# Small products of the late runs of tokens placed further behind their DVE steps in a fused gated scan and top-1 expert layer

## The chip, the cores and the metric

One core of a Trainium2 chip runs the whole kernel. The metric is the device time of one execution in microseconds (us). Engines: PE is TensorE (PEld are its weight loads), DVE is VectorE, ACT is ScalarE, POOL is GpSimd, SP is SyncE, which here only issues DMAs (SPq in the rows).

## What is computed

Inputs are x, r_gate and i_gate of 4 x 5056 x 256 floats, a modality per token, and 8 experts with w1 (256 x 1024) and w2 (1024 x 256).

```python
# gated scan over time, for each of 4 batches and 256 channels
a_t = exp(8 * sigmoid(r_gate) * log(a_base))
x_gated = sqrt(max(1 - a_t * a_t, 1e-6)) * sigmoid(i_gate) * x
h = a_t[:, t] * h + x_gated[:, t];  y[:, t] = h          # t = 0..5055
# top-1 experts on the 20224 rows of y
logits = y @ w_gate + modality_bias[modality_id]
e = argmax(logits);  gate = softmax(logits)[e]
out = gate * (relu(y @ w1[e]) @ w2[e])
```

## The kernel before

**Two stages that overlap.** The first stage goes over 23 runs of time steps (`CHUNKS`, numbered 0 to 22; runs 4 to 20 have 256 steps, that is 1024 tokens over the four batches). For each run it loads the three inputs, does the scan, finds a power of two that scales the run's rows into f16 (`size_chunk`, "scale"), splits the scaled rows into a high and a low f16 half (`split_chunk` on ACT, `low_parts` on DVE), multiplies by the gate weights ("logits", at the end of `low_parts`), finds each token's expert and its rank among that expert's tokens (`route_chunk`, "ranks"), transposes the rows by DMA (`rows_part`, line 858) and scatters them by POOL into the experts' lists in HBM (line 1043). The second stage takes pages of 256 rows of the two likeliest experts, and a few pages of 128, back from there (tile X, line 1280), multiplies them by w1 (L1371, into ph), makes relu halves H on ACT (L1302) and on DVE (L1304), multiplies by w2 (L1411, into po), scales on ACT (L1323) and scatters the output by POOL (L1327). The main products stand on PE in groups of twelve of 128 x 256; a page of 256 rows has four groups into ph and four into po, so one H step of DVE goes with two groups. There are 654 such groups in all.

**The small products.** Each run has few of them on PE, and each one sits between DVE steps. Scale: DVE makes `mxy` (L774); PE turns it into psz (L633); DVE reduces psz (`m1y`, L636) and makes `dmy` (L640); PE spreads that (L644, L646); DVE makes the scales `scy` (L653) from `miy` (L649), and ACT's and DVE's split wait for these. Logits: the last DVE low step (L817), then sixteen products (L830), then DVE `lt` (L889) and the steps of routing. Ranks: DVE `cu` (L922), then three products (L927 to L930), then DVE `dt` (L934). psz and psl, the PSUM tiles of scale and of logits with ranks, share two buffers (tag `lg`).

**What sets the order.** Every engine works through its own queue in program order. The order is written while the kernel is built, by a planner (`run`) that has a cost for every step. A piece of work is a generator; it asks for an engine, a duration, a condition and a lag, and the step that it asked for is put in the queue of the engine when the planner's clock of that engine reaches it. The lag of a request is the least time in the plan between the end of this step and the start of the *next* step of the same generator; without one it is 0.1 (same engine) or 0.2 (another engine):

```python
lag = th.req[3] if len(th.req) > 3 else None
th.req = next(th.gen, None)          # puts the step into its queue
th.t += (0.1 if th.req[0] == eng else 0.2) if lag is None else lag
```

So the lag on a request for PE holds back the DVE step that reads the product, and the lag on a DVE request holds back the product that follows it. Runs 7 and 8 and later ones have 3.0 for the lag between L633 and `m1y` and between L644 and `miy` (`SIZE_LAG`), and 3.0 between the last low step and the logits, between `cu` and the ranks and between the ranks and `dt` (`LAG`). Between `mxy` and L633 and between `dmy` and L644 there is no lag but the 0.2.

Of the kernel before, what the change touches and what calls it, by code (L numbers as in the profile page):

```python
# [49 lines left out]
C_STEP = 2.89  # L50
GROW = 1.01
SIZE_LAG = 3.0
EARLY = 7
URGENT = 0.03
ROW_STEP = 2.4
LAG = 3.0
# [21 lines left out]
def place(kind, c):  # L78

    return BASE[kind] + C_STEP * c + (RANK[kind][c] if c < len(RANK[kind]) else 0.0)  # L80
# [7 lines left out]
def columns(c):  # L88

    return B * CHUNKS[c][1] // P  # L90
# [16 lines left out]
def kernel(  # L107
# [161 lines left out]
    def seen(*names):  # L269
        return allof(*[lambda n=n: mark.get(n, FAR) for n in names])  # L270

    def room(tag, k=1):

        def at():
            d = slots[tag]
            old = [n - d.bufs for n in range(d.n, d.n + k) if n >= d.bufs]
            return max((d.back.get(n, FAR) for n in old), default=0.0)
        return at

    def take(tag):  # L280
        slots[tag].n += 1
        return slots[tag].n - 1

    def give(tag, n):
        slots[tag].back[n] = plan["end"]

    def allof(*fs):
        def at():
            t = 0.0
            for f in fs:  # L290
                t = max(t, f())
                if t >= FAR:
                    break
            return t
        return at
# [6 lines left out]
    def add(gen, prio, t=0.0, urgent=False):  # L302

        th = Thread(gen, prio, t, urgent)
        if th.req is not None:
            threads.append(th)
# [258 lines left out]
    def done(c, name):  # L565

        give(*tickets[c, name])
# [62 lines left out]
    def power_of_two(name, mx, ng, ps, sc, iv, lag=None):  # L630

        yield "PE", 0.1, None, lag
        nc.tensor.matmul(ps[0:ng, 0:P], mx, identb, start=True, stop=True)  # L633
        yield "DVE", 0.2, None
        m1 = sm.tile([4, 1], F32, name=f"m1{name}", tag="m1")
        nc.vector.tensor_reduce(out=m1[0:ng], in_=ps[0:ng, 0:P], axis=AX.X, op=ALU.max)  # L636
        yield "DVE", 0.14, None
        dm = sm.tile([4, 5], BF16, name=f"dm{name}", tag="dm")
        nd = ng if ng == 1 else ng + 1
        nc.vector.tensor_scalar(  # L640
            out=dm[0:ng, 0:nd], in0=identx[0:ng, 0:nd], scalar1=m1[0:ng], scalar2=None, op0=ALU.mult
        )
        yield "PE", 0.1, None, lag
        nc.tensor.matmul(ps[:, P : P + ng], onesb[0:ng, :], dm[0:ng, 0:ng], start=True, stop=True)  # L644
        if nd > ng:
            nc.tensor.matmul(ps[:, P + ng : P + nd], quad, dm[:, ng:nd], start=True, stop=True)  # L646
        yield "DVE", 0.1, None
        mi = sm.tile([P, 5], I32, name=f"mi{name}", tag="mi")
        nc.vector.tensor_scalar(  # L649
            out=mi[:, 0:nd], in0=ps[:, P : P + nd].bitcast(I32), scalar1=EBITS, scalar2=None, op0=ALU.bitwise_and  # L650
        )
        yield "DVE", 0.1, None, 0.0
        nc.vector.scalar_tensor_tensor(  # L653
            out=sc.bitcast(I32), in0=mi[:, 0:ng], scalar=6.0 * TWO23, in1=s256[:, 0:ng], op0=ALU.max, op1=ALU.subtract,
            reverse1=True,
        )
        yield "DVE", 0.1, None, 0.0
        nc.vector.tensor_scalar(
            out=iv.bitcast(I32), in0=mi[:, nd - 1 : nd], scalar1=6.0 * TWO23, scalar2=-4.0 * TWO23, op0=ALU.max, op1=ALU.add,
        )  # L660
# [75 lines left out]
    def modality_bias(c):  # L736

        C = columns(c)
        yield "POOL", 0.3 + 0.03 * C, seen(("modality", c))
        shc = [P, C, E]  # L740
        mc = slice(COL[c], COL[c + 1])
        bm = sm.tile([P, C, E], F32, name=f"bm{c}", tag="bm", bufs=3)
        bn = sm.tile([P, C, E], F32, name=f"bn{c}", tag="bn")
        mul = lambda o, a, m: nc.gpsimd.tensor_tensor(
            out=o, in0=a[:, mc].broadcast_to(shc), in1=mb[:, m : m + 1, :].broadcast_to(shc), op=ALU.mult
        )
        mul(bm, mf, 1)
        mul(bn, mg, 0)
        nc.gpsimd.tensor_tensor(out=bm, in0=bm, in1=bn, op=ALU.add)
        tiles["bm", c] = bm  # L750
        mark["bias", c] = plan["end"] + 0.2

    def size_chunk(c):

        t0, T = CHUNKS[c]
        z = T / 256
        yield "DVE", 0.07 + 2.13 * z, seen(("load", c, "x"))
        xg = tiles[c][2].rearrange("p (h g t) -> p h g t", h=2, g=B)
        top = sm.tile([P, B], F32, name=f"top{c}", tag="top", bufs=4)
        nc.vector.tensor_reduce(  # L760
            out=top, in_=xg.rearrange("p h g t -> p g h t"), axis=AX.XY, op=ALU.max, apply_absolute_value=True
        )
        mark["peak", c] = plan["end"] + 0.2
        mx = sm.tile([P, 4], BF16, name=f"mxy{c}", tag="mxy", bufs=4)
        grow = GROW * T ** 0.5
        if c:
            yield "DVE", 0.12, seen(("scan", c - 1))
            lm = sm.tile([P, B], F32, name=f"lm{c}", tag="lm")
            nc.vector.tensor_reduce(
                out=lm, in_=tiles["last", c - 1].rearrange("p h g o -> p g (h o)"), axis=AX.X, op=ALU.max,  # L770
                apply_absolute_value=True,
            )
            yield "DVE", 0.1, None
            nc.vector.scalar_tensor_tensor(out=mx, in0=top, scalar=grow, in1=lm, op0=ALU.mult, op1=ALU.add)  # L774
        else:
            yield "DVE", 0.1, None
            nc.vector.tensor_scalar(out=mx, in0=top, scalar1=grow, scalar2=None, op0=ALU.mult)
        yield "SP", 0.0, allof(room("lg"), seen("gate")), 0.0
        lag = SIZE_LAG if c > 6 else SIZE_LAG / 3 if c > 1 else None
        tl = take("lg")  # L780
        ps = psl.tile([P, 512], F32, name=f"psz{c}", tag="lg")
        sc = sm.tile([P, 4], F32, name=f"scy{c}", tag="scy", bufs=4)
        iv = sm.tile([P, 1], F32, name=f"ivy{c}", tag="ivy", bufs=4)
        yield from power_of_two(f"y{c}", mx, B, ps, sc, iv, lag)
        give("lg", tl)
        yield "DVE", 0.1, None, 0.0
        ivl = sm.tile([P, 1], F32, name=f"ivl{c}", tag="ivl", bufs=4)
        nc.vector.tensor_tensor(out=ivl, in0=iv, in1=ivg, op=ALU.mult)
        tiles["iv", c] = iv, ivl
        tiles["sc", c] = sc  # L790
        mark["sized", c] = plan["end"] + 0.2

    def split_chunk(c):
# [6 lines left out]
        ys = a.rearrange("p (s h k g b) -> p s h g k b", s=2, h=2, g=B, b=Q)  # L800
        add(low_parts(c, yg, ys, sc), (0, place("low", c)), plan["end"], urgent=c < EARLY)
        add(modality_bias(c), (0, place("low", c)), plan["end"])
# [7 lines left out]
    def low_parts(c, yg, ys, sc):  # L810

        t0, T = CHUNKS[c]
        z = T / 256
        lag = LAG if c > 6 else None
        for g in range(B):
            yield "DVE", 0.14 + 0.52 * z, seen(("high", c, g)), 0.0 if g < B - 1 else lag
            nc.vector.scalar_tensor_tensor(  # L817
                out=ys[:, 1, :, g], in0=yg[:, :, g, :].rearrange("p h (k b) -> p h k b", b=Q), scalar=sc[:, g : g + 1],
                in1=ys[:, 0, :, g], op0=ALU.mult, op1=ALU.subtract,
            )  # L820
        mark["split", c] = plan["end"] + 0.2
        done(c, "g")
        yield "PE", 0.35 + 0.35 * z, room("lg"), 1.25 if c > 6 else 0.0
        tl = take("lg")
        ps = psl.tile([P, 512], F32, name=f"psl{c}", tag="lg")
        tiles["ps", c] = tl, ps
        mm = [(s, h) for s in range(2) for h in range(2)]
        for m, (s, h) in enumerate(mm):
            for g in range(B):
                nc.tensor.matmul(  # L830
                    ps[Q * g : Q * g + Q, 0:T], wg16[:, h, :], ys[:, s, h, g], start=(m == 0), stop=(m == len(mm) - 1),
                )
        mark["lg", c] = plan["end"]
        y_free(c)
# [46 lines left out]

    def route_chunk(c):
        C = columns(c)
        lag = LAG if c > 6 else None
        small = 0.1 + 0.014 * C
        yield "DVE", 0.07 + 0.27 * C / 8, seen(("lg", c), *([("oh", c - 1)] if c else []))
        ticket, ps = tiles["ps", c]
# [19 lines left out]
        nc.vector.tensor_tensor(out=l, in0=l, in1=mx.broadcast_to(sh), op=ALU.subtract)  # L907
        add(gates(c, l), (0, place("gates", c)), plan["end"] + 0.2, urgent=c < EARLY)
        yield "DVE", small, None
# [513 lines left out]
    def start_chunk(c):  # L1423
        early = c < EARLY
        add(load_chunk(c), (0, place("load", c)))
# [91 lines left out]
```

## Time and profile before

| what | value |
|---|---|
| median of three runs | 968.93 us (964.12 to 969.37) |
| the profiled execution, its own time | 970.96 us |
| its span, first to last instruction | 969.2 us |
| mean granted TensorE clock | 0.988 |
| busy: PE, PEld, DVE, ACT, POOL | 909.6, 787.4, 650.7, 578.6, 427.8 us |

Busy times are of the span; what lies around it is 1.8 us. Matmuls are pipelined, so a PE that is shown busy all the time can still do less than its peak; a wait of PE shows as idle time in front of an instruction, with the instruction that ended it. "PEclk" in tables by stretch is the granted clock, 1.00 for 2.4 GHz.

### The profile page before, as it was taken

How to read it: one execution, taken by the hardware profiler on the slowest of the kernel's cores; microseconds unless marked ns; L12 is line 12 of the kernel's file. 1: busy time of each engine (PE TensorE's matmuls, PEld its weight loads, DVE VectorE, ACT ScalarE, POOL GpSimd, SP SyncE). 2: the span in 40 equal slices, each digit the busy share in tenths (PEclk: the TensorE clock that was granted, in tenths of full speed). 3: DMA queues.
4: the chain of work that ended last, by engine and by line, in shares of the span. 5: the costliest groups of instructions: out<-in, count | busy, mean ns of one | idle time of the engine just before them, and what ended most of it. 6: DMA issues, size and time to landing. Idle time of an engine off the chain costs nothing. (4 is left out here: it accounts for less than half of the span.)

```text
span 969.2 us, 22535 instructions
## 1 busy us (share of the span) xinstructions
PE 909.6 (94%) x8518; PEld 787.4 (81%) x8518; DVE 650.7 (67%) x1665; ACT 578.6 (60%) x819; POOL 427.8 (44%) x550
## 2 busy tenths in 40 slices
PE   3968998998999999998999999999999999999996
PEld 2556787787888888887888888888998988888886
DVE  7978988688898788798979876973352332233321
ACT  8978667696768766866787676843233333333332
POOL 6434356345456555544555555444443212112112
PEclk9998999899999999999999999999999999999999
DMA  9587798889779888998988887643732222122110
GB/s 317 155 221 207 178 215 263 184 211 246 226 164 218 183 230 210 230 204 179 232 228 221 209 196 202 138 94 93 175 106 72 53 51 60 45 51 60 45 40 19
DMA packets 227992, 155.85 MB, mean 161 GB/s; under 512 B 197857, under 2 KB 201058, under 8 KB 227874
## 3 DMA queue, kind: packets, MB, share of 16 engines
q1 hardware_dynamic: 211554, 110.35, 51.0%
q0 software_dynamic: 16176, 43.98, 13.5%
q8 instruction: 68, 1.11, 0.5%
q14 instruction: 50, 0.41, 0.2%
q10 hardware_dynamic: 144, 0.00, 0.0%
HBM read 68.76 MB, written 44.35 MB: 117 GB/s over the span
## 5 line engine op out<-in xcount | busy, mean ns | idle before, releaser
L1371 PE MATMUL ph<-X,hw 128*128 128x256 f16 (+1 forms) x3840 | 469.3, 273 | 14.8 <-DMA X<-rows 14.1
L1411 PE MATMUL po<-hw,H 128*128 128x256 f16 x3840 | 473.9, 274 | 6.0 <-ACT H L1302 4.8
L1371 PEld LDWEIGHTS <-hw 128*128 128x128 f16 x3936 | 377.3, 98 | 64.4 <-DMA X<-rows 11.3
L1411 PEld LDWEIGHTS <-H 128*128 128x128 f16 x3864 | 374.5, 98 | 54.4 <-ACT H L1302 5.5
L1304 DVE SCALAR_TENSOR_TENSOR H<-ph,H 128x512 f16<-128x512 f32 (+1 forms) x332 | 219.9, 668 | 246.1 <-ACT H L1302 244.8
L1302 ACT ACTIVATE H<-ph 128x512 f16<-128x512 f32 (+1 forms) x332 | 190.8, 581 | 255.1 <-PE ph L1371 253.1
L1327 POOL DMA_INDIRECT out_dram<-ot,mt x161 | 178.3, 1107 | 276.7 <-ACT ot L1323 238.2
L1043 POOL DMA_INDIRECT rows<-rt,di x158 | 178.2, 1128 | 225.5 <-PE ph L1371 86.8
L1323 ACT ACTIVATE ot<-po,gt 128x256 f32<-128x256 f32 x161 | 76.1, 473 | 74.3 <-PE po L1411 72.1
L622 DVE TENSOR_TENSOR_SCAN g<-a,g 128x512 f32<-128x512 f32 (+1 forms) x78 | 94.8, 1227 | 0.5
L605 DVE SCALAR_TENSOR_TENSOR g<-x,g 128x1024 f32<-128x1024 f32 (+1 forms) x40 | 48.4, 1209 | 24.2 <-ACT x L600 24.2
L817 DVE SCALAR_TENSOR_TENSOR a<-g,scy,a 128x512 f16<-128x512 f32 (+2 forms) x92 | 60.0, 676 | 4.7 <-ACT a L805 4.7
L805 ACT ACTIVATE a<-g,scy 128x512 f16<-128x512 f32 (+2 forms) x92 | 56.3, 656 | 4.4 <-DVE scy L653 4.4
L594 ACT ACTIVATE a<-a,ch 128x1024 f32<-128x1024 f32 (+2 forms) x46 | 50.9, 1118 | 0.1
L588 ACT ACTIVATE a<-a 128x2048 f32<-128x2048 f32 (+2 forms) x23 | 38.4, 1671 | 20.2 <-DMA a<-in_r_gate_dram 20.1
L579 DVE SCALAR_TENSOR_TENSOR g<-g,x 128x1024 f32<-128x1024 f32 (+1 forms) x40 | 48.0, 1200 | 0.1
L760 DVE TENSOR_REDUCE top<-x 128x4 f32<-128x2048 f32 (+2 forms) x23 | 45.3, 1971 | 3.7 <-DMA x<-in_x_dram 3.7
L573 ACT ACTIVATE g<-g 128x2048 f32<-128x2048 f32 (+2 forms) x23 | 38.4, 1668 | 13.1 <-DMA g<-in_i_gate_dram 13.0
L598 ACT ACTIVATE x<-a 128x2048 f32<-128x2048 f32 (+2 forms) x23 | 38.4, 1669 | 11.2 <-DVE g L579 7.1
L600 ACT ACTIVATE x<-x,quarter 128x2048 f32<-128x2048 f32 (+2 forms) x23 | 40.6, 1763 | 0.3
L600 ACT ACT_TABLE_LOAD x22 | 28.2, 1283 | 0.4
L1043 POOL DMA_INDIRECT rows<-nt,ni x16 | 15.8, 990 | 20.8 <-PE ph L1371 9.2
(210 smaller groups left out, 463.5 us busy)
## 6 DMA issues: line engine op xcount, KB each, us to landing
a<-in_r_gate_dram SPq DMA_DIRECT2D x38, 512.0 KB
g<-in_i_gate_dram SPq DMA_DIRECT2D x38, 512.0 KB
x<-in_x_dram SPq DMA_DIRECT2D x38, 512.0 KB
wr<-in_moe_w_dram SPq DMA_DIRECT2D x4, 1024.0 KB
out_dram<-ot,mt POOLq DMA_INDIRECT x161
rows<-rt,di POOLq DMA_INDIRECT x158
cr<-in_moe_w_dram SPq DMA_DIRECT2D x2, 1024.0 KB
rt<-a SPq DMA_TRANSPOSE x92
```

The costliest lines, as they stand in the source:

```text
L594: nc.scalar.activation(sl, sl, AF.Exp, scale=ch[:, h : h + 1], bias=ch[:, h : h + 1])
L600: nc.scalar.activation(s, s, AF.Sqrt, scale=-0.25, bias=quarter)
L622: nc.vector.tensor_tensor_scan(out=gi, data0=ai, data1=gi, initial=0.0, op0=ALU.mult, op1=ALU.add)
L805: nc.scalar.activation(ys[:, 0, :, g], yg[:, :, g, :].rearrange("p h (k b) -> p h k b", b=Q), AF.Copy, scale=sc[:, g : g + 1])
L817: nc.vector.scalar_tensor_tensor(out=ys[:, 1, :, g], in0=yg[:, :, g, :].rearrange("p h (k b) -> p h k b", b=Q), scalar=sc[:, g : g + 1], i ...
L1043: ins = nc.gpsimd.indirect_dma_start(out=rows[:, :], out_offset=bass.IndirectOffsetOnAxis(ap=idx, axis=0), in_=src, in_offset=None, bounds ...
L1302: nc.scalar.activation(t.H[:, 0, hs, :], ph[:, :, 0:st], AF.Relu)
L1304: nc.vector.scalar_tensor_tensor(out=t.H[:, 1, hs, :], in0=ph[:, :, 0:st], scalar=0.0, in1=t.H[:, 0, hs, :], op0=ALU.max, op1=ALU.subtract,)
L1323: nc.scalar.activation(t.ot[:, a, :], po, AF.Copy, scale=t.gt[:, a : a + 1])
L1327: ins = nc.gpsimd.indirect_dma_start(out=out[:, :], out_offset=bass.IndirectOffsetOnAxis(ap=t.mt[:, a, 0:1], axis=0), in_=t.ot[:, a, :], i ...
L1371: ins = nc.tensor.matmul(ph[:, v, 0:st], lhsT, rhs, start=(m == 0), stop=(m == len(mm) - 1))
L1411: ins = nc.tensor.matmul(po, lhsT, rhs, start=(f == 0 and m == 0), stop=(f == NF - 1 and m == len(mm) - 1))
```

## The change

From run 9 on, the lag behind each scale product becomes 12.0 in place of 3.0, and the lag on the last low step, on `cu` and on the rank products becomes 6.0 in place of 3.0. No instruction of PE, DVE, POOL or SP is added or taken away; ACT has 43 table loads in place of 47 in its queue, by the order in which its functions follow each other.

```diff
 SIZE_LAG = 3.0
+SIZE_LATE = 12.0
+LATE = 9
+LAG_LATE = 6.0
...
-        lag = SIZE_LAG if c > 6 else SIZE_LAG / 3 if c > 1 else None
+        lag = SIZE_LATE if c >= LATE else SIZE_LAG if c > 6 else SIZE_LAG / 3 if c > 1 else None
...
-        lag = LAG if c > 6 else None
+        lag = LAG_LATE if c >= LATE else LAG if c > 6 else None
...
-        lag = LAG if c > 6 else None
+        lag = LAG_LATE if c >= LATE else LAG if c > 6 else None
```

Lines of the changed kernel are 3 higher than those of the kernel before (L1304 is L1307). Up to run 9's `m1y` on DVE all queues are the same. Counted in PE's queue, this many groups of main products stand ahead of the products of a run, before and after:

| run | L633 | L644 | logits | ranks |
|---|---|---|---|---|
| 9 | 121, 121 | 128, 136 | 144, 156 | 153, 167 |
| 10 | 137, 137 | 144, 155 | 162, 188 | 170, 197 |
| 13 | 203, 211 | 206, 225 | 223, 245 | 236, 256 |
| 16 | 267, 295 | 270, 305 | 288, 326 | 301, 337 |
| 17 | 289, 322 | 292, 339 | 311, 372 | 318, 383 |
| 18 | 313, 349 | 317, 362 | 333, 380 | 340, 388 |
| 19 | 335, 350 | 338, 362 | 356, 389 | 361, 401 |
| 22 | 401, 436 | 405, 446 | 414, 462 | 419, 469 |

Page 26 starts behind group 200 and page 30 behind group 232 in both. Between `mxy` of run 9 and `mxy` of run 16 DVE's queue holds 73 H steps before and 87 after; from run 16 to run 19 it holds 34 and 27, from run 19 to run 22 32 and 43.

DVE's queue at run 9's `m1y` (the reduction of the first scale product; g9 is run 9's scan tile, H16 and H17 are pages 16 and 17, cu8 and b8 belong to run 8), before:

```order
L922 SCALAR_TENSOR_TENSOR cu8_3934<-rmask8_189,oh8_3917 128x64
L636 TENSOR_REDUCE m1y9_3952<-psz9_3885 4x1
L605 SCALAR_TENSOR_TENSOR g9_3161<-x9_3225,g9_3161 128x1024
L1304 SCALAR_TENSOR_TENSOR H16_3865<-ph16_0_3866,H16_3865 128x512
L1304 SCALAR_TENSOR_TENSOR H16_3865<-ph16_1_3921,H16_3865 128x512
L1032 TENSOR_REDUCE sg8_3994<-ex8_3957 128x8
```

and after:

```order
L967 TENSOR_REDUCE b8_4156<-bh8_4151 1x2
L1307 SCALAR_TENSOR_TENSOR H17_4041<-ph17_1_4088,H17_4041 128x512
L639 TENSOR_REDUCE m1y9_4160<-psz9_3885 4x1
L763 TENSOR_REDUCE top10_4175<-x10_3738 128x4
L1307 SCALAR_TENSOR_TENSOR H17_4041<-ph17_2_4135,H17_4041 128x512
L643 TENSOR_SCALAR dmy9_4228<-identx_171,m1y9_4160 4x5
```

`m1y` of run 9 moved back by 31 rows, behind the rest of run 9's scan, and `dmy` went with it.

DVE's queue ahead of run 16's `mxy` (a15 and g15 are run 15's tiles; L817 and L820 are the low steps, L760 and L763 the peak of x), before:

```order
L817 SCALAR_TENSOR_TENSOR a15_6269<-g15_6545,scy15_6900,a15_6269 128x16x32
L1304 SCALAR_TENSOR_TENSOR H33_7151<-ph33_2_7238,H33_7151 128x512
L817 SCALAR_TENSOR_TENSOR a15_6269<-g15_6545,scy15_6900,a15_6269 128x16x32 x3
L1304 SCALAR_TENSOR_TENSOR H33_7151<-ph33_3_7280,H33_7151 128x512
L760 TENSOR_REDUCE top16_7338<-x16_7190 128x4
L1304 SCALAR_TENSOR_TENSOR H34_7317<-ph34_0_7318,H34_7317 128x512
L1315 TENSOR_SCALAR gt33_7377<-mt33_6743,hiv1_230 128x2
L1142 TENSOR_TENSOR d36_7380<-b13_6751,u_136 1x2
L769 TENSOR_REDUCE lm16_7382<-last15_7233 128x4
```

and after:

```order
L1307 SCALAR_TENSOR_TENSOR H36_7547<-ph36_1_7585,H36_7547 128x512
L1307 SCALAR_TENSOR_TENSOR H36_7547<-ph36_2_7646,H36_7547 128x512
L1307 SCALAR_TENSOR_TENSOR H36_7547<-ph36_3_7681,H36_7547 128x512
L1318 TENSOR_SCALAR gt36_7761<-mt36_7304,hiv0_229 128x2
L1307 SCALAR_TENSOR_TENSOR H37_7732<-ph37_0_7733,H37_7732 128x512
L1307 SCALAR_TENSOR_TENSOR H37_7732<-ph37_1_7769,H37_7732 128x512
L763 TENSOR_REDUCE top16_7814<-x16_7694 128x4
L1307 SCALAR_TENSOR_TENSOR H37_7732<-ph37_2_7801,H37_7732 128x512
L652 TENSOR_SCALAR miy15_7850<-psz15_7290 128x5
L772 TENSOR_REDUCE lm16_7855<-last15_7607 128x4
```

The low steps of run 15 moved from ahead of run 16's peak to behind run 16's `mxy`, and H steps of the pages stand alone there.

SP's queue at the load of page 26 (X26; rt11 and rt10 are transposes of runs 11 and 10, a13, g13 and x13 the loads of run 13), before:

```order
L1281 DMA mt25_5241<-rows_78 128x2x2
L858 DMA_TRANSPOSE rt11_0_5300<-a11_4015 128x8x128 x4
L1267 TENSOR_LOAD sel14_5449
L1267 ISA x2
L1280 ISA
L1280 DMA_TRANSPOSE X26_5498<-rows_78 128x4x256
```

and after:

```order
L861 DMA_TRANSPOSE rt10_0_4970<-a10_3585 128x8x128
L540 DMA a13_5411<-in_r_gate_dram 128x1024 x2
L540 DMA g13_5473<-in_i_gate_dram 128x1024 x2
L540 DMA x13_5537<-in_x_dram 128x1024
L861 DMA_TRANSPOSE rt11_0_5574<-a11_4011 128x8x128
L1270 TENSOR_LOAD sel14_5556
```

Five loads of run 13 now stand between the load of page 25 and that of page 26, and only one of run 11's four transposes is ahead of it.

## Rows read from the trace of the kernel before

**Rows 1.** The page, busy time by engine over the span.

```profile
PE 909.6 (94%) x8518; PEld 787.4 (81%) x8518; DVE 650.7 (67%) x1665; ACT 578.6 (60%) x819; POOL 427.8 (44%) x550
```

**Rows 2.** Busy time by engine in four stretches (us from the span's start; length, then busy and count of PE, PEld, DVE, ACT, POOL; granted clock; share of the DMA engines; GB/s).

```profile
240.00:450.00 210.00, 200.33 (x1906) 174.54 (x1906) 181.53 (x437) 152.26 (x198) 116.56 (x117) 1.00 0.88 209
450.00:545.00 95.00, 94.47 (x883) 81.78 (x883) 83.30 (x197) 69.97 (x89) 51.09 (x54) 0.98 0.88 216
545.00:634.00 89.00, 89.00 (x840) 78.08 (x840) 72.03 (x178) 61.69 (x88) 45.18 (x47) 1.00 0.74 178
700.00:900.00 200.00, 200.00 (x1875) 179.77 (x1873) 67.03 (x157) 65.16 (x117) 49.81 (x52) 1.00 0.26 65
```

**Rows 3.** Waits of PE, by what ended them (total us, times, longest), asked for the stretches 240 to 260, 260 to 300, 300 to 340, 340 to 400, 400 to 440 and 440 to 460 us, in this order; 460 to 660 us has none.

```profile
PE psz L633 <- DVE mxy L774: 2.3, 1, 2.3
...
PE psz L644 <- DVE dmy L640: 1.5, 1, 1.5
PE psz L633 <- DVE mxy L774: 0.2, 1, 0.2
...
PE psz L644 <- DVE dmy L640: 0.7, 1, 0.7
...
PE psz L633 <- DVE mxy L774: 2.3, 2, 1.6
PE psz L644 <- DVE dmy L640: 0.9, 1, 0.9
...
PE psz L633 <- DVE mxy L774: 1.5, 1, 1.5
...
PE psz L633 <- DVE mxy L774: 2.6, 1, 2.6
```

**Rows 4.** The logits' products (L830) and the rank products (L928) over the whole span: durations, and until what PE or PEld sat idle before them ("issue" is no wait that the profile shows).

```profile
L830 PE MATMUL psl<-a,wg x368: 206/273/314, 29.4 to 652.6; 128*32 128x256 f16 x136, 128*32 128x128 f16 x32, 128*32 128x96 f16 x16
its engine sat idle before it (us, times) until:
  issue: 5.3, 22
...
L928 PE MATMUL psl<-cu,ones x23: 173/193/193, 34.1 to 659.3; 128*128 128x64 f16 x17, 128*128 128x32 f16 x4, 128*128 128x24 f16 x2
...
  DVE cu L922: 0.4, 1
```

**Rows 5.** The ten us behind the longest of these waits, busy time by engine and granted clock as in rows 2.

```profile
450.00:460.00 10.00, 9.59 (x73) 7.74 (x74) 8.13 (x28) 6.58 (x7) 2.94 (x3) 0.83 0.79 137
```

**Rows 6.** Instructions in order of time before run 16's scale product, of ACT, of DVE and of PE (start, us, engine, line, operation; in brackets the idle time before it and what ended it).

```profile
438.50 1.91 ACT L573 ACTIVATE g<-g 128x2048 f32<-128x2048 f32 x1 [1.31 <-DMA g<-in_i_gate_dram]
...
437.22 0.69 DVE L1304 SCALAR_TENSOR_TENSOR H<-ph,H 128x512 f16<-128x512 f32 x1 [0.87 <-ACT H L1302]
...
440.93 0.69 DVE L1304 SCALAR_TENSOR_TENSOR H<-ph,H 128x512 f16<-128x512 f32 x1 [1.45 <-ACT H L1302]
...
446.67 2.27 DVE L760 TENSOR_REDUCE top<-x 128x4 f32<-128x2048 f32 x1
...
450.22 0.14 DVE L774 SCALAR_TENSOR_TENSOR mxy<-top,lm 128x4 bf16<-128x4 f32 x1
...
450.41 0.27 PE L633 MATMUL psz<-identb,mxy 128*4 128x128 bf16 x1 [2.62 <-DVE mxy L774]
```

**Rows 7.** DVE's H steps between 250 and 550 us, grouped (count, busy us, mean ns, idle before them).

```profile
L1304 DVE SCALAR_TENSOR_TENSOR H<-ph,H 128x512 f16<-128x512 f32 x106 | 71.4, 678 | 15.3 <-ACT H L1302 14.9
```

**Rows 8.** PE in order of time, two groups of twelve main products that follow each other, and the start of the next.

```profile
257.88 1.47 PE L1371 MATMUL ph<-X,hw 128*128 128x256 f16 x12
259.19 1.47 PE L1411 MATMUL po<-hw,H 128*128 128x256 f16 x12
260.50 0.71 PE L1371 MATMUL ph<-X,hw 128*128 128x256 f16 x5
```

**Rows 9.** In order of time: the rank product of run 9 and the last scatter of its rows, the same of run 10, the last scatter of run 7 and the load of page 18 that waits for it.

```profile
285.62 0.19 PE L927 MATMUL psl<-oh,um 128*128 128x64 f16 x1
...
317.60 0.98 POOL L1043 DMA_INDIRECT rows<-rt,di  x1 [1.67 <-PE po L1411]
...
309.21 0.19 PE L927 MATMUL psl<-oh,um 128*128 128x64 f16 x1
...
348.39 1.39 POOL L1043 DMA_INDIRECT rows<-rt,di  x1 [2.96 <-DMA x<-in_x_dram]
...
250.13 1.78 POOL L1043 DMA_INDIRECT rows<-rt,di  x1 [1.12 <-PE po L1411]
...
254.88 1.28 SPq L1280 DMA_TRANSPOSE X<-rows  x1
```

**Rows 10.** SP and PE in order of time around the longest wait for a page (page 10), and the waits of PE for pages between 50 and 150 us and between 150 and 250 us.

```profile
164.49 2.18 SPq L537 DMA_DIRECT2D g<-in_i_gate_dram  x2
167.60 1.41 SPq L1280 DMA_TRANSPOSE X<-rows  x1
...
171.90 2.74 PE L1371 MATMUL ph<-X,hw 128*128 128x256 f16 x12 [5.89 <-DMA X<-rows]
...
PE ph L1371 <- DMA X<-rows: 7.4, 4, 4.0
...
PE ph L1371 <- DMA X<-rows: 6.7, 2, 5.9
```

## The prediction

> **What bounds the kernel now.** I read the page's engine rows first: PE is busy for 94% of the span, no other engine for more than 67% [rows 1], so the question is where PE waits, not who is busy. Then the table by stretch [rows 2], split at the places where the change acts: all queues are the same up to run 9's first small product at about 240 us, and run 22's last one stands at about 660 us. PE is idle for 9.7 us of the 210 between 240 and 450 us, for 0.5 of the next 95 and not at all from 545 us to 634 and from 700 to 900. The reader is to see that the whole loss that this change can touch lies in one stretch.
>
> What PE waits for there are DVE's small steps [rows 3]: 2.3 + 0.2 + 2.3 + 1.5 + 2.6 = 8.9 us before L633, for `mxy`, and 1.5 + 0.7 + 0.9 = 3.1 us before L644, for `dmy`. Run 9's own 2.3 us come before the first changed row and stay. That leaves 9.7 us. Logits and ranks, which the change also moves, have nothing of the sort: L830 only shows issue times of 0.2 us each, and L928 waited once, for 0.4 us, in the whole span [rows 4]. The longest wait also costs clock: in the 10 us behind it the granted clock is 0.83 of 2.4 GHz [rows 5], that is a part of the time at 1.2 GHz, and 10 x 0.17 = 1.7 us are lost. So 9.7 + 1.7 = 11.4 us can be won at most, 1.2% of the time.
>
> Why is DVE late? Before run 16's product [rows 6], ACT waited 1.31 us for a load, its H step came later for that, DVE stood 0.87 and 1.45 us without work, and from there to `mxy` at 450.22 its queue had no gap in which to catch up: low steps, the peak of x (2.27 us) and H steps follow each other. DVE is busy 181.5 us of the 200.3 that PE works in this stretch, 91%; between 450 and 545 us 83.3 of 94.5, 88%, and PE lost nothing; then 72.0 of 89, 81% [rows 2]. So a DVE at 91% turns each disturbance into a wait of PE, and at 88% or less it has not done so here.
>
> **The change part by part.**
>
> *The lag stands behind the products that wait.* A lag on a PE request holds back the DVE step that reads the product. L633 still stands 0.2 behind `mxy`, and L644 0.2 behind `dmy`, so no wait of [rows 3] is met directly. The lags that do stand ahead of products (logits, ranks) go to products that don't wait. By themselves they give 0. They cost nothing either: the steps held back have no reader on PE before the logits.
>
> *What it does instead is to stretch the first stage.* `scy` comes later by two lags, the split waits for it, and each run's logits and ranks follow. Run 22's rank product stands behind 469 groups in place of 419, and the same DVE work is spread over more of PE's. A group takes 1.31 us, from start to start [rows 8]; an H step of DVE goes with two, and takes 0.673 us, 71.4 us over 106 [rows 7].
>
> From run 9 to run 16 there are 87 H steps in place of 73: PE gets 14 x 2.62 = 36.7 us more work, DVE 14 x 0.67 = 9.4 us more. DVE's share goes from 181.5 / 200.3 to 190.9 / 237.0, 81%. That is the share of the stretch from 545 us, where PE waited for nothing [rows 2]. I take 0.3 us for what is left of the 11.4 there, with ends 0 and 3 (run 9 to run 11 stay close: 137 and 165 groups for their L633).
>
> From run 16 to run 19 it goes the other way: 27 H steps in place of 34. PE loses 7 x 2.62 = 18.3 us of its 94.5 and has 76.2; DVE has 83.3 - 4.7 = 78.6, 103%. Here DVE cannot keep up. By the nearest row, the stretch at 91% lost 11.4 us in 200, 5.7%, which is 4.3 us of 76. The ends are 0, if what run 18 needs is ready early (its `mxy` stands 29 rows ahead of run 19's, its product only just ahead of run 19's), and 4.3 + 2.4 = 6.7 with the shortfall of 2.4 us added. I take 4.3. From run 19 to run 22 it is 43 H steps for 32, light again: 0.
>
> *Pages come later to PE.* Whatever a run's chain issues moves with it: sixteen logits products and three rank products on PE, four transposes on SP, eight scatters on POOL. The rows of run 9 are the last that page 26 may need, those of run 10 the last for page 30. From run 9's rank product to the last scatter of its rows take 317.6 - 285.6 = 32.0 us; from the last scatter of run 7 to the load that waited for it 254.9 - 250.1 = 4.8 [rows 9]; from a page's load to its first product 171.9 - 167.6 = 4.3 [rows 10]. Page 26 starts behind group 200; run 9's ranks stood behind 153 and now stand behind 167. 33 groups are 43.2 us, the chain is 32.0 + 9.1 = 41.1: 2.1 us to spare. For run 10, 348.4 - 309.2 = 39.2 us and 9.1 are 48.3; its ranks move from 170 to 197, page 30 is behind 232, and 35 groups are 45.9 us: short by 2.4, if POOL again takes 39.2 us; with run 9's 32.0 us there are 4.8 to spare. Such waits are in the trace: 14.1 us in six, the longest 5.89 [rows 10]. There SP's queue had a burst of loads ahead of the page's load, as it now has before pages 26 and 30. I take 1.0 us for the two, with ends 0 and 11.8. SP's other entries pay nothing: the loads come earlier against PE or wait for buffers that no product needs at once.
>
> *The two psz and psl buffers* are held for two lags more; the next L633 or L830 waits for one in the plan, so PE finds it free. After run 22, 654 - 469 = 185 groups, 242 us, are left for the last pages and for the cold experts' weights, which now come later too: 0. ACT's four table loads less lie beside idle time of ACT: 0.
>
> The sum: -11.4 + 0.3 + 4.3 + 1.0 = -5.8 us. Against the profiled execution's own 970.96 us that is 965.2; it is 2.0 us above the median of 968.93, so the forecast for the median is 968.93 - 5.8 = **963.1 us**.
>
> A second look at the 11.4: PEld is busy 174.5 of 210 us in the lossy stretch, 83.1%, and 179.8 of 200 us between 700 and 900, 89.9% [rows 2]; a deficit of 6.8% of 210 is 14.2 us. That PE's matmul rows look fuller than they are is what the Trainium skill says too (Perfetto Trace Analysis, Identifying the Most-Contended Engine): matmul occupancy is not a good measure of PE, the busy share of LDWEIGHTS is. By that rule the sum would be -14.2 + 5.6 = -8.6 us.
>
> **The rivals.**
>
> *The waits only move* (0.25). What speaks for it: the lag is on the wrong side of the products that wait, 6.6 us of the 9.7 fall before L633 by single disturbances (a late load [rows 6]), and those stay. Against it: the same two products waited for nothing from 460 us on [rows 3], with the same tables. The stretch would lose its 11.4 us again, and with 1.0 for pages the time is 968.93 + 1.0 = 969.9, between 966 and 972.
>
> *Pages run dry, and it gets slower* (0.13). The mechanism is above: page 30, and page 26 behind its burst of five loads, start later than PE gets to them. It decides once run 10's last scatter comes later than 9.1 us before PE is at group 232. Each wait is then like the one at 171.90, 5.89 us, and the twelve products behind it took 2.74 us in place of 1.47, so 1.3 more: 2 x 7.2 = 14.4, with 4.3 and 0.3 this is 19.0 - 11.4 = +7.6, **976.5 us**. Against it: in this stretch DVE and POOL are less pressed, and five of six such waits were far shorter.
>
> *More comes back than the waits show* (0.10). The deficit of PEld is the loss, 14.2 us, short gaps between products included: 968.93 - 8.6 = 960.3 us. For it: a stretch at full pace gives 89.9%. Against it: small products take their own time on PE in every run, and that is part of the deficit. The Trainium skill's rule above is the reason to keep it.
>
> **How the numbers follow.** The forecast has 0.52, with 957.5 (all 11.4 us) and 968 as its own ends. What a measurement of this kernel tells from no change is about 0.5%, 4.8 us: faster is below 964.1, slower above 973.8. The forecast stands close to the bound; I put three quarters of it below, by the stretch at 81% and the free places of page 26: 0.39 faster, 0.13 the same. The moved waits give 0.01, 0.21 and 0.03, pages that run dry 0.02 same and 0.11 slower, the deficit 0.10 faster. Sums: 0.50 faster, 0.36 the same, 0.14 slower. The range goes from 957, all of the 11.4 us, to 971, which leaves out the dry pages and the upper end of the moved waits.
>
> **What the profile after would show.** Right: between run 9's and run 16's products PE waits for under 1.5 us before L636 and L647 (the two lines in the changed kernel), DVE's share there is about 81%, and the granted clock is 1.00. A cluster of waits before these lines falls between runs 16 and 19, near 4 us in all. The first stage ends some 60 us later. Pages 26 and 30 wait for 1 us or less. Wrong: waits of 1 to 3 us before L636 at runs 12 to 16 as before (the waits only move), or waits of PE for X near 350 and 395 us (dry pages), or new waits of the main products for H, which none of these terms holds.

## The result, and the profile after

| | before | after |
|---|---|---|
| median | 969.15 us (14 runs) | 975.95 us (971.30 to 980.69, 14 runs) |
| the profiled execution, its own time | 970.96 us | 977.94 us |
| its span, mean granted clock | 969.2 us, 0.988 | 976.1 us, 0.981 |

The ratio is 1.0076, with an interval of 1.0053 to 1.0099: slower, by 7 us. The prediction said 963.1 us, 957 to 971, so it was wrong in the sign. Lines of the changed kernel are 3 higher (L636 is L633, L647 is L644, L1374 is L1371).

The page of the profile after, busy time by engine, answers [rows 1]. PE is busy 6 us longer for the same 8518 products, and its weight loads (PEld) 3 us; no other engine is:

```profile
PE 915.5 (94%) x8518; PEld 790.6 (81%) x8518; DVE 650.0 (67%) x1665; ACT 572.2 (59%) x815; POOL 424.8 (44%) x550
```

The first three stretches of [rows 2] (busy and count of PE, PEld, DVE, ACT, POOL; granted clock; DMA share; GB/s), and PE's waits of over 0.5 us in all in the stretches 240 to 450 and 450 to 634 us (total, times, longest):

```profile
240.00:450.00 210.00, 201.42 (x1861) 173.82 (x1859) 162.34 (x394) 133.92 (x181) 95.17 (x102) 0.97 0.73 177
450.00:545.00 95.00, 91.80 (x860) 80.14 (x858) 73.64 (x162) 69.92 (x86) 44.80 (x46) 1.00 0.88 215
545.00:634.00 89.00, 87.90 (x839) 76.68 (x837) 72.53 (x185) 55.54 (x82) 40.63 (x43) 1.00 0.71 179
```

```profile
PE psz L636 <- DVE mxy L777: 4.6, 1, 4.6
PE ph L1374 <- DMA X<-rows: 3.9, 2, 3.4
...
PE psz L636 <- DVE mxy L777: 3.2, 3, 2.1
PE psz L647 <- DVE dmy L643: 0.8, 2, 0.5
```

In the first stretch PE is idle for 8.6 us, which is less than the 9.7 of before. But the many small waits of [rows 3] have become two large ones, and the clock, 1.00 before, is 0.97: 210 x 0.03 = 6.3 us, give or take 1 for the rounding. Idle time and clock over the three stretches are 8.6 + 6.3 + 3.2 + 1.1 = 19.2 us after, and 9.7 + 0.5 + 1.9 = 12.1 before. The difference is 7.1; the two executions differ by 6.98. So the table holds the loss as far as its rounding tells. Not all of the 6.3 us belongs to the change. Some 0.8 us lie ahead of 316 us (granted clock 0.95 from 300 to 316), most of it while PE stood idle anyway, and 1.3 us lie in the first ten us, behind the wait of 2.18 us before run 9's own scale product (239.04 us), ahead of every changed row:

```profile
240.00:250.00 10.00, 10.00 (x84) 8.51 (x82) 7.77 (x20) 7.11 (x9) 3.28 (x4) 0.87 0.87 245
```

About half of the difference is clock, the rest idle time.

**The first large wait** is before run 12's scale product. SP, ACT, DVE and PE of the kernel after, in order of time on each (start, us, engine, line; in brackets the idle time before and what ended it):

```profile
294.29 0.35 SPq L540 DMA_DIRECT2D a<-in_r_gate_dram  x1
...
297.52 0.47 SPq L540 DMA_DIRECT2D a<-in_r_gate_dram  x1
298.03 5.58 SPq L540 DMA_DIRECT2D g<-in_i_gate_dram  x2
304.53 2.37 SPq L540 DMA_DIRECT2D x<-in_x_dram  x2
...
303.45 1.91 ACT L591 ACTIVATE a<-a 128x2048 f32<-128x2048 f32 x1 [4.11 <-DMA a<-in_r_gate_dram]
...
305.88 0.69 DVE L1307 SCALAR_TENSOR_TENSOR H<-ph,H 128x512 f16<-128x512 f32 x1 [6.32 <-ACT H L1305]
...
311.87 2.29 DVE L763 TENSOR_REDUCE top<-x 128x4 f32<-128x2048 f32 x1 [1.85 <-DMA x<-in_x_dram]
...
315.57 0.16 DVE L777 SCALAR_TENSOR_TENSOR mxy<-top,lm 128x4 bf16<-128x4 f32 x1
...
315.78 0.27 PE L636 MATMUL psz<-identb,mxy 128*4 128x128 bf16 x1 [4.63 <-DVE mxy L777]
315.98 2.74 PE L1414 MATMUL po<-hw,H 128*128 128x256 f16 x12
```

and SP's loads for the same run in the kernel before:

```profile
282.94 0.83 SPq L537 DMA_DIRECT2D a<-in_r_gate_dram  x2
...
303.66 1.50 SPq L537 DMA_DIRECT2D x<-in_x_dram  x2
```

The load of `a` is issued 11.4 us later than before, g and x queue behind it on SP, ACT stands 4.11 us for the load, DVE 6.32 us for ACT and 1.85 for x, and then `mxy` is late. Meanwhile run 12's product has moved forward in PE's queue: it stands behind 173 groups where it stood behind 180, the one run for which it moves that way. Run 12's x is issued 6.6 us before PE reaches the product (304.53 to 311.15); before it was 18.8 (303.66 to 322.5, without a wait). From the issue of x to `mxy` take 11.0 us, so it cannot be in time. Against PE both count: x itself is issued only 0.9 us later than before, and the product stands 11.3 us earlier, so x would have to come earlier too. The held load keeps it from that; what x does without the hold, own_a12 shows below.

**The second** is page 26. SP, POOL and PE of the kernel after, and SP's waits between 285 and 365 us (total, times, longest):

```profile
339.65 0.83 SPq L540 DMA_DIRECT2D a<-in_r_gate_dram  x2
343.99 1.97 SPq L540 DMA_DIRECT2D g<-in_i_gate_dram  x2
349.00 0.33 SPq L540 DMA_DIRECT2D x<-in_x_dram  x1
351.51 1.25 SPq L861 DMA_TRANSPOSE rt<-a  x1
354.16 2.15 SPq L1283 DMA_TRANSPOSE X<-rows  x1
...
346.28 1.01 POOL L1046 DMA_INDIRECT rows<-rt,di  x1 [0.67 <-PE ph L1374]
...
359.29 2.74 PE L1374 MATMUL ph<-X,hw 128*128 128x256 f16 x12 [3.38 <-DMA X<-rows]
```

```profile
SPq L540 <- PE psl L833: 12.6, 1, 12.6
SPq L540 <- DMA a<-in_r_gate_dram: 9.4, 3, 4.7
SPq L540 <- DMA rt<-a: 5.8, 2, 3.4
```

The five loads of run 13 stand ahead of page 26's. The first waits 12.6 us for a product of line 833: the logits of run 10 (338.7 to 339.1 us), the last readers on PE of the tile that run 13's `a` is to take. Tile `a` has three buffers. It carries a run from its gate values through the split halves to the logits and the transposes, so run 12 takes run 9's buffer and run 13 run 10's. In the same way the 3.4 us on `rt<-a` is run 12's load of `a`, which waits for run 9's transposes. The kernel before has no wait of SP on either in this stretch. The last scatter of run 9, at 346.28, is not what page 26 waits for: by the 4.8 us of [rows 9] its load could have gone at 351.1.

**The clock.** The twenty us behind each wait, columns as in [rows 2]:

```profile
316.00:336.00 20.00, 20.00 (x161) 16.59 (x161) 13.27 (x26) 9.65 (x12) 8.14 (x9) 0.87 0.46 106
359.00:379.00 20.00, 19.71 (x182) 16.75 (x183) 13.11 (x39) 5.30 (x11) 7.29 (x8) 0.92 0.82 192
```

2.6 us are lost behind the first, 1.6 behind the second; twelve products take 2.74 us at both places in place of 1.47 [rows 8]. So the first wait costs 7.2 us and the second 5.0.

### The profile page after: what moved, and what is told of

It is laid out like the page before. It is cut to its first block, busy times and chain, and to the rows that moved or that the text cites. A ratio compares the mean times of both kernels' runs of the same rounds, so it can differ in the third digit from the quotient of the medians.

```text
span 976.1 us, 22516 instructions
## 1 busy us (share of the span) xinstructions
PE 915.5 (94%) x8518; PEld 790.6 (81%) x8518; DVE 650.0 (67%) x1665; ACT 572.2 (59%) x815; POOL 424.8 (44%) x550
## 5 line engine op out<-in xcount | busy, mean ns | idle before, releaser
L1374 PE MATMUL ph<-X,hw 128*128 128x256 f16 (+1 forms) x3840 | 471.6, 274 | 17.2 <-DMA X<-rows 15.5
L1374 PEld LDWEIGHTS <-hw 128*128 128x128 f16 x3936 | 379.6, 99 | 69.5 <-DMA X<-rows 11.5
L1307 DVE SCALAR_TENSOR_TENSOR H<-ph,H 128x512 f16<-128x512 f32 (+1 forms) x332 | 219.6, 667 | 237.4 <-ACT H L1305 196.3
L820 DVE SCALAR_TENSOR_TENSOR a<-g,scy,a 128x512 f16<-128x512 f32 (+2 forms) x92 | 59.8, 672 | 4.7 <-ACT a L808 3.3
L763 DVE TENSOR_REDUCE top<-x 128x4 f32<-128x2048 f32 (+2 forms) x23 | 45.4, 1973 | 6.7 <-DMA x<-in_x_dram 6.6
```

The costliest lines, as they stand in the source:

```text
L820: nc.vector.scalar_tensor_tensor(out=ys[:, 1, :, g], in0=yg[:, :, g, :].rearrange("p h (k b) -> p h k b", b=Q), scalar=sc[:, g : g + 1], i ...
L1307: nc.vector.scalar_tensor_tensor(out=t.H[:, 1, hs, :], in0=ph[:, :, 0:st], scalar=0.0, in1=t.H[:, 0, hs, :], op0=ALU.max, op1=ALU.subtract,)
L1374: ins = nc.tensor.matmul(ph[:, v, 0:st], lhsT, rhs, start=(m == 0), stop=(m == len(mm) - 1))
```

## The experiments

Theory: **the longer lags hold tile `a`**, and SP's queue hands that on to the scale product of run 12 and to page 26. Rivals: the moved steps and products cost by themselves; or only the nearer place of run 12's product does. Ratios are to the kernel before on the same chip (its medians were 962.8 to 967.7 us).

**own_a12.** All five queues as after, but run 12's `a` has a buffer of its own, so that runs 13 to 15 too take a buffer that is given back one run earlier:

```diff
+own = c == 12 and name == "a"
-... tag=tag, bufs=BUFS[tag])
+... tag="aown" if own else tag, bufs=1 if own else BUFS[tag])
```

> The changed kernel with every queue in the same order, but run 12's tile a (the r_gate tile that is later split into f16) gets a buffer of its own, so run 12's first load no longer waits for the transposes of run 9, and run 13's takes the buffer that run 9 left and no longer waits for the logits of run 10. Held-buffer theory (the lags keep a run's tile a until later logits and transposes, so loads start late and in a burst, and what stands behind them on SP, ACT and DVE comes late): run 12's loads come some 3 us earlier and its scale product waits 0 to 2 us in place of 4.63; run 13's loads come at about 325 us in place of 340, the wait for page 26 (3.38 us at 359 us) is gone, no clock falls behind it; 6 to 12 us faster than the changed kernel, 964 to 970 us. Late-rows theory (page 26 waits since the scatters of run 9 come later): its wait stays at 2 to 4 us, and the time stays at 974 to 977.

Measured: 967.64 us, 1.003 [0.9992, 1.0067]. First stretch of [rows 2], issue of run 12's x on SP, and PE's waits from 300 to 400 us (lines 6 higher than before):

```profile
240.00:450.00 210.00, 204.43 (x1938) 178.47 (x1936) 168.20 (x406) 138.28 (x186) 101.79 (x106) 1.00 0.75 183
```

```profile
298.41 2.33 SPq L543 DMA_DIRECT2D x<-in_x_dram  x2
```

```profile
PE psz L639 <- DVE mxy L780: 3.6, 2, 2.0
PE ph L1377 <- DMA X<-rows: 2.0, 2, 1.4
```

By the medians one buffer takes some 60% of the loss away, with every instruction in its place; what is left is between -0.08 and 0.67%, which just meets the change's 0.53 to 0.99%. The x of run 12 is issued 10.8 us before PE reaches the product in place of 6.6; the wait there is 2.0 us, and the clock stays at 1.00. Page 26 waits for 1.4 us in place of 3.4, where it had been expected not to wait.

**no_pace.** Order as after; from run 12 on a load no longer waits on SP for the load two before it.

```diff
-                if c >= PACED:
+                if PACED <= c < 12:
```

> The changed kernel with every queue in the same order, but from run 12 on a load no longer waits on SP for the landing of the load two before it. Held-buffer theory: page 26's load comes after a burst that is issued in 2 us in place of 10, so its wait of 3.38 us goes or halves; run 12's scale product still waits 3 us or more, since its loads come in one burst that the DMA engines take 14 us to move; 970 to 975 us. If pacing alone made both waits, both go and the time is 962 to 967. Late-rows theory: both stay, 974 to 977.

Measured: 967.93 us, 1.0018 [0.9984, 1.0051]. Without the pacing run 12's product waits 1.44 us, page 26 0.67, though the held buffer still stops SP for 8.9 and 7.3 us. That run 12's product would still wait 3 us or more, and the time be 970 or more, was a miss: the pacing is a full link of the chain, since what is held late is also spread out. In this execution a long wait stands at run 13's product in their place, for the second half of its x, which is issued at 358.21 us:

```profile
368.05 0.27 PE L636 MATMUL psz<-identb,mxy 128*4 128x128 bf16 x1 [3.89 <-DVE mxy L777]
```

**size_only and lag_only**, one half of the change each (`LAG_LATE = 3.0`; `SIZE_LATE = 3.0`).

> The changed kernel with LAG_LATE back at 3: only the lags behind the scale products are longer. Run 12's product stands 26 in place of 9 planned us behind its last load, and pages 26 and 30 are free. Held-buffer theory: the two big losses are gone, and the stretched first stage leaves few waits of PE: 961 to 967 us. Late-rows theory: rows still come later by two lags of 9: pages 26 and 30 wait, 972 or more.

> The changed kernel with SIZE_LATE back at 3: only the lags ahead of logits and ranks and behind ranks are longer. Held-buffer theory: run 12's product keeps its place of before and no page is tight; the waits before L633 and L644 are about those of before, 966 to 971 us. If the lags ahead of products were what gained, it is faster than before by 5 us or more.

Measured: 968.61 us, 1.0038 [1.0010, 1.0066], and 966.68 us, 0.9995 [0.9972, 1.0018]. By the medians the lag of scale has half the loss, the lag of logits and ranks none alone. Neither gains anything. That size_only would be at 961 to 967 us was a miss. Its profile has neither of the two large waits, but 3.5 us before L647 of run 11 (321.2 us): run 12's load of `a` still waits on SP for run 9's transposes, ACT stands 2.3 us for that load, DVE 3.6 for ACT and 2.4 for x, and the late DVE step is now `dmy` of run 11. So the hold can reach PE at another product.

**runs_9_10 and from_11**: the long lags for two runs only (`LATE <= c < 11`), and for all but these (`LATE = 11`).

> The long lags for runs 9 and 10 alone, 3 as before from run 11 on. All queues are as in the changed kernel up to run 11's first changed step, so run 12's loads wait for run 9's tile and run 12's scale product stands as close to them as there. Held-buffer theory: this part holds the loss: run 12's product waits 3 to 5 us near 312 us with the clock at 1.2 GHz for a while behind it, page 26 waits 1 to 4 us near 355; slower than before by 0.3 to 1%. Lag-itself theory (fourteen runs with long lags each cost a little): two of fourteen runs give a seventh of the loss, no difference from before.

> The long lags from run 11 on: runs 9 and 10 give their tiles back as before. Held-buffer theory: run 12's product and pages 26 and 30 wait for nothing; the first stage is still stretched (run 22's logits near the place of the changed kernel), DVE is less busy up to run 16, so few waits before L633 and L644; 0.4 to 1% faster than before. Lag-itself theory: twelve fourteenths of the loss, 0.5% slower or more.

Measured: 975.53 us, 1.0093 [1.0064, 1.0121], and 970.98 us, 1.0039 [1.0013, 1.0065]. Two runs of tokens cost as much as the whole change, and they are those whose tiles runs 12 and 13 take. But the waits of 3 to 5 us at run 12 and of 1 to 4 at page 26, expected for runs_9_10, came only in part. PE's waits there from 300 to 360 us:

```profile
PE psz L647 <- DVE dmy L643: 3.4, 2, 2.1
PE ph L1374 <- DMA X<-rows: 1.0, 1, 1.0
PE psz L636 <- DVE mxy L777: 0.5, 1, 0.5
```

SP stands for run 9's transposes again (4.0 us at most), ACT 2.4 us for the load of `a`, DVE 4.5 us for ACT; the 3.4 us are at runs 11 and 12, and no clock falls behind them. This execution took 973.29 us, the shortest of four, and does not account for the whole 0.93%. That from_11 would be faster was a miss too: without the held tiles of runs 9 and 10 it is still slower, by 0.13 to 0.65%. So the long lags cost something from run 11 on as well. The longest waits of from_11 are 2.4 us each, at runs 16 and 17; what makes them is open.

**lag_ahead.** The kernel before, with 3.0 on the two steps that PE was seen to wait for, `mxy` and `dmy`, from run 9 on: the lag put where the prediction said that this change does not put it.

```diff
-yield "DVE", 0.1, None                          # mxy
+yield "DVE", 0.1, None, 3.0 if c >= 9 else None
-yield "DVE", 0.14, None                         # dmy
+yield "DVE", 0.14, None, 3.0 if ... >= 9 else None
```

> The kernel before, with a lag of 3 us on the DVE steps that feed L633 and L644 from run 9 on, so that these products themselves stand 3 us behind their steps; the lags of before elsewhere. If PE's waits are single late DVE steps of 0.2 to 2.6 us, a product 3 us further behind meets nearly all of them: waits before these two lines go from 9.7 to under 2 us with no fall of the clock, 0.6 to 1.1% faster than before. If the waits only move (DVE at 91% late by more each time), no difference.

Measured: 968.53 us, 1.0007 [0.9978, 1.0036]. PE's waits from 240 to 634 us:

```profile
PE psz L633 <- DVE be L939: 3.7, 2, 2.8
PE po L1411 <- DVE H L1304: 2.7, 4, 1.0
PE psl L830 <- DVE be L939: 2.6, 1, 2.6
```

The waits for `mxy` and `dmy` are gone, and others have come that were not there: for `be`, the last step that reads the ranks of an earlier run in a buffer that psz and psl share, and for H. Here the waits only move, as the first rival of the prediction said.

**r12_later.** After, with 8.0 on `mxy` of run 12, so that its product moves back.

```diff
-yield "DVE", 0.1, None
+yield "DVE", 0.1, None, 8.0 if c == 12 else None
```

> The changed kernel with one lag more: run 12's scale product stands 8 us behind the step that feeds it, in place of 0.2. Its loads stay as late as in the changed kernel. Held-buffer theory: the 4.63 us wait at that product and the fall of the clock behind it, 7.6 us together, go; page 26 stays tight and may wait 1 to 4 us; 968 to 971 us. If the late loads hold PE up in another way too (H steps behind the ACT step that waits for a load), waits of the main products for H take its place and the time stays at 973 or more.

Measured: 972.06 us, 1.0051 [1.0027, 1.0075]. PE's waits from 240 to 634 us show that the 4.6 before L636 at run 12 is gone, and that waits of 2.1 us for `be`, before run 10's logits, and of 1.4 us for `dmy` of run 11 stand near its old place (the 2.2 before L636 are run 9's own):

```profile
PE psz L636 <- DVE mxy L777: 2.9, 3, 2.2
PE psl L833 <- DVE be L942: 2.1, 1, 2.1
PE psz L636 <- DVE be L942: 2.1, 1, 2.1
```

By the medians the near place of run 12's product may have a third of the loss; the interval overlaps that of the change, and the order behind it changes too (run 13's product stands behind 195 groups in place of 211).

**before_again and after_again**: both kernels unchanged, one more execution of each in the profile.

> The kernel before, unchanged, looked at once more, to see how much of the 11.4 us of waits and clock that the prediction counted belongs to the kernel and how much to that one execution (970.96 us, when most executions since took 966 to 968). Theory (each execution has its own late loads, the order only decides which of them reach PE): waits at other products than before, 8 to 13 us lost behind run 9's product, time 964 to 973. Rival (the waits are fixed by the order): the same 2.3 us before L633 near 322 us and 2.6 us near 450 us again.

> The changed kernel, unchanged, looked at once more. Theory (the held tile a makes run 12's product and page 26 late in every execution): waits of over 2 us at L636 near 315 us and of over 2 us for X of page 26 near 359 us again, each with a granted clock near 0.9 behind it, time 972 to 979. Rival (it was one bad execution): neither wait over 1 us again, and another place in their stead.

Measured: 961.51 and 973.54 us. First stretch and PE's waits from 240 to 634 us of the kernel before:

```profile
240.00:450.00 210.00, 205.29 (x1955) 178.83 (x1954) 187.51 (x452) 154.57 (x201) 117.19 (x118) 1.00 0.88 212
```

```profile
PE psz L633 <- DVE mxy L774: 3.3, 4, 1.1
PE psz L644 <- DVE dmy L640: 1.3, 1, 1.3
```

First stretch and PE of the kernel after:

```profile
240.00:450.00 210.00, 201.95 (x1873) 174.82 (x1874) 164.62 (x398) 134.86 (x183) 98.00 (x103) 0.98 0.74 179
```

```profile
315.13 0.26 PE L636 MATMUL psz<-identb,mxy 128*4 128x128 bf16 x1 [3.94 <-DVE mxy L777]
315.32 2.74 PE L1414 MATMUL po<-hw,H 128*128 128x256 f16 x12
...
357.96 2.60 PE L1374 MATMUL ph<-X,hw 128*128 128x256 f16 x12 [2.66 <-DMA X<-rows]
```

The two waits of after come back at the same places, with their half clock. Those of before don't come back in size: 4.6 us in place of 9.7 (run 9's own, 2.3 and 2.2 us, left out in both), none over 1.3, no clock lost. That 8 to 13 us would be lost, at other products, was a miss: the waits stand before products of runs 10, 13, 15 and 16, which waited in the first profile too, and they are smaller or no larger. The prediction had counted an execution with more late loads than this one: between 240 and 455 us ACT stood 15.7 us for them there, 9.9 here.

**own_unpaced and own_unpaced_b**: own_a12 and no_pace together, in the order of after and in that of before.

> The order of the changed kernel, with both of what each removed the loss alone: run 12's tile a has its own buffer, and from run 12 on no load waits on SP for the load two before it. If the held buffer and the paced loads are one chain, the second removes nothing that the first left: 967 to 969, within 2 us of own_a12's ratio of 1.003. If they are two causes of some 4 us each that add up, 961 to 965, faster than the kernel before.

> The kernel before with the same two edits (own buffer for run 12's tile a, no pacing from run 12), to see whether they help without the long lags. Theory (before's loads for a are not late, since run 10's logits come 26 groups earlier there): within 2 us of the kernel before, ratio 0.998 to 1.002. Rival (the two edits make any order faster by 1%): 957 to 960.

Measured: 965.75 us, 1.0020 [0.9993, 1.0047], and 964.12 us, 0.9997 [0.9981, 1.0013]. Together the edits do no more than each alone, as far as intervals of 0.3% either way tell: one chain, not two causes. And they don't help an order that holds nothing. No kernel of this study is shown to beat the one before.

**own_a13.** Order as after; run 13's `a` has its own buffer (`c == 13`), so the hold by the logits of run 10 is gone and the one by run 9's transposes stays.

> The order of the changed kernel; run 13's tile a has its own buffer, so that run 13's loads don't wait for the logits of run 10, while run 12's still wait for the transposes of run 9. Theory (two holds, each with its own price): the wait of 4 to 5 us at run 12's product stays, with its clock, and the wait for page 26's X goes; about half of the loss is left, 3 to 5 us over the kernel before, ratio 1.003 to 1.005. Rival (only the hold of run 12 costs, page 26 is late for its sake): nothing is gained, ratio 1.0065 to 1.009. Rival (the logits of run 10 are the whole cause): ratio 1.000 to 1.002 and no wait of over 2 us near 315 us.

Measured: 966.76 us, 1.0036 [1.0011, 1.0062]. PE's waits from 300 to 400 us, and the longest of SP from 285 to 365 us:

```profile
PE psz L639 <- DVE mxy L780: 5.4, 2, 4.3
PE ph L1377 <- DMA X<-rows: 1.4, 2, 1.3
```

```profile
SPq L864 <- DMA rows<-rt,di: 11.8, 1, 11.8
```

About half of the loss is left, with the wait of 4.3 us at run 12. The first theory stands: two holds, each with its price. Page 26 waits for 1.3 us still. What SP stands for now is a scatter; run 9's last goes at 339.55 us and page 26's load at 345.34, 5.8 us behind it where [rows 9] had 4.8, so here the rows themselves come late.

**r9_10_own.** The order of runs_9_10, with the own buffer of own_a12.

> Long lags for runs 9 and 10 alone, in the order that runs_9_10 had (ratio 1.0093 [1.0064, 1.0121]), but with a buffer of its own for run 12's tile a. Theory (the long lags of runs 9 and 10 cost only by holding that tile): ratio 0.998 to 1.003. Rival (they cost by the moved DVE steps and products themselves): 1.006 to 1.010 again.

Measured: 965.54 us, 1.0028 [1.0003, 1.0054], where runs_9_10 had 1.0093. The intervals don't meet: with the same order, two thirds of that loss were the held buffer. What remains, 0.03 to 0.54%, may be the moved steps themselves, the rival's cause; it stays open.

## Why the prediction was wrong, point by point

**What can be won: 11.4 us.** Mis-sized. The waits were read rightly, but from one execution. In the three stretches of [rows 2] the same kernel lost 12.1 us in the first profile and 4.8 in the second. The order sets the products before which PE waits; how long it waits differs with the late loads of the one execution.

**The lag stands behind the products that wait: 0.** Right: no product was met by its own lag. lag_ahead, with the lags on the other side, won nothing either.

**The first stage is stretched, and DVE's share falls.** Right. Run 22's last rank product comes at 731.0 us, 71.7 later than before; DVE is busy 162.3 of the 201.4 us that PE works in the first stretch, 81%, and 184.2 of 234.3, 79%, from 247 to 492 us, run 9 to run 16, for which 81% was forecast. That this would leave 0.3 us of waits, with an end of 3, was wrong: there are 4.6 at run 12 and 2.6 of clock behind them. A DVE with time to spare still starts late if ACT waits for a load. The busy share said how a disturbance is made good, and nothing of what disturbs.

**SP's other entries pay nothing.** This is the step that failed: it put these loads at nothing. The prediction said of them: "the loads come earlier against PE or wait for buffers that no product needs at once". Run 12's load waited for run 9's transposes, and run 12's product came 6.6 us behind its x; run 13's waited 12.6 us for run 10's logits, with page 26 behind it on SP. In place of 0 the wait at run 12 costs 7.2 us, and that at page 26, for which the pages' term has 1.0, costs 5.0. own_a12, own_a13 and r9_10_own show the hold. The prediction counted psz and psl, which the lags hold, but not `a`, which the held split, logits and transposes hold. The table of groups left out run 12, the one whose product had come nearer, so that its load came later against PE and not earlier.

**The two psz and psl buffers: 0.** Nearly right: one wait of 0.34 us for `be`, at run 20. But it is a hold of the same kind; in lag_ahead, from_11 and r12_later the longest such waits are 2.8, 2.4 and 2.1 us.

**Runs 16 to 19: 4.3 us, ends 0 and 6.7.** Right in place, too large: three waits, 3.3 us in the first profile (2.14, 0.62 and 0.52) and 1.9 in the second (0.64, 0.69, 0.52). DVE was busy 93% of PE's time there (70.9 of 76.4 us between 492 and 570), not 103%.

**Pages 26 and 30: 1.0 us, ends 0 and 11.8.** 3.4 and 0.55 us, and 1.6 of clock: within the ends. The rival of dry pages had named page 26 behind its burst of five loads, and 976.5 us; the time fits, the mechanism half. The loads made page 26 late by 3.1 us (354.16 against 351.1), the scatters by little; with the hold gone (own_a12, own_a13, own_unpaced) 1.3 to 1.9 us are left, in own_a13 behind the scatters. The other half was run 12. Of the six waits for pages that the rival was weighed by, one of the five called far shorter is 4.0 us [rows 10].

**The rivals.** With the hold gone (own_a12, own_unpaced) the time is not told from that of the kernel before, and idle time and clock in the three stretches are 7.1 and 7.2 us, between the two profiles of before. So the change without the hold looks like the rival in which the waits only move. That more comes back than the waits show, nothing here bears out: PEld was busy for 178.8 of the 210 us in the second profile of before, 4.3 more than in the first. Against 89.9% of 210 it still lacks 10.0 us, where waits of PE and clock show 4.7. The stretch from 545 to 634 us, where PE waits for nothing but small products still run, is the nearer measure: 78.1 of 89 us, 87.7% [rows 2]. Against that the first profile lacks 9.7 us and the second 5.4, close to their waits, so some 5 us of the 14.2 were no loss. The Trainium skill's measure (Perfetto Trace Analysis, Identifying the Most-Contended Engine) follows the waits here, but its distance from a stretch without small products is no sum to be won.

## What to carry to other kernels

Before a step is held back, list the tiles that it is the last to read, the loads that take those buffers next, and what stands behind these loads on their queue: a lag that costs nothing on its own engine can be paid for three runs later by another. For each product compare the time from its load to its place in the queue with what the chain between them takes (here 11.0 us, against 18.8 before and 6.6 after). Take what can be won from two profiled executions at least: the same waits came to 9.7 us in one and 4.6 in another.

## What was not expected of the hardware

The two long waits of PE cost about half as much again in clock: 2.6 us behind 4.63, 1.6 behind 3.38. Twelve products took 2.74 us behind each of these and behind 3.94 us in the second profile, 2.60 behind 2.66, where 1.47 is their time at 2.4 GHz; the clock was at its lower level, 1.2 GHz, there. In own_a12, where PE waited 2.0 us at the same product, and in the second profile of before, the granted clock was 1.00 from 240 to 450 us. A wait of the same size went the other way before run 9's own product, in the first profile of the kernel after,

```profile
239.04 0.22 PE L636 MATMUL psz<-identb,mxy 128*4 128x128 bf16 x1 [2.18 <-DVE mxy L777]
239.19 2.73 PE L1414 MATMUL po<-hw,H 128*128 128x256 f16 x12
```

while in the second twelve products took 1.48 us behind 2.24. In this case two long waits cost more than many small ones: 8.6 us idle after, with 4.2 of clock behind the two, against 9.7 before with 1.7, all of it behind its longest, 2.62 us [rows 5].
